# P V in four bursts per pair of heads, with no maxima in those steps

## The chip, the cores and the metric

The kernel runs on one core of one Trainium2 chip. A core has a matrix engine (TensorE, PE in the profile, with its weight loads shown apart as PEld), VectorE (DVE), ScalarE (ACT), GpSimd (POOL) and a queue for transfers (SyncE, SP). Each engine works through its own instructions in the order in which the program lists them, and waits for the others by semaphores. The metric is the device time of one execution in microseconds (us); three runs of the kernel before gave 1525.46, 1531.42 and 1532.0.

## What is computed

Attention with pooled queries, and behind it a mixture of experts with one expert per token:

```
q_pool = q.reshape(B, H, S // 2, 2, D).mean(axis=3)         # B=8, H=8, S=1152, D=64: 576 queries a head
scores = matmul(q_pool, k.transpose(0, 1, 3, 2)) / sqrt(D)
scores = scores - max(scores, axis=-1, keepdims=True)
attn   = exp(scores); attn = attn / (sum(attn, axis=-1) + 1e-9)
x      = matmul(attn, v)        # to [4608, 512]; then argmax gate, w1, relu, w2 and two gate factors per token
```

The change is in the attention, which takes the first 1020 us of some 1530; what follows is the experts' part, which the change does not touch.

## The kernel before

**The stages.** The 64 heads are worked off as 32 pairs, and the pairs one behind the other. A pair takes 18 steps: a step is one of the 9 key chunks of 128 keys of one of its two heads, so step 0 to 8 belong to the first head and 9 to 17 to the second (`s` in the code counts the steps of all pairs, and "step 4" below is `s % 18 == 4`). Three things run through the steps at different places of the program at once:

- *scores*: in each step the scores of this step's chunk, keys on the partitions and 576 queries in two halves of 288. Four matmuls of 288 columns (two at L394, two at L396) fill one of two PSUM buffers (`sps0`, `sps1`, by turns). The exponentials follow in one of two ways. On the GpSimd way ScalarE writes exp twice, once in f32 (`p32`, L408) and once in f16 (`ph`, L409), and GpSimd writes their difference, the low half `pl`, at L410. On the VectorE way (chunks listed in `PLP`) ScalarE writes `ph` (L400) and then exp over the scores in PSUM (L401), and VectorE takes the difference at L404 straight from PSUM. On this way the PSUM buffer comes free only after L404; on the other it comes free after L409. The scores two steps on need that buffer.
- *maxima*: for the *next* pair, the row maxima, 27 units a pair. A unit is two matmuls (three in some) of 384 columns at L331 into one of three small PSUM buffers, and a reduce by VectorE at L332. After 15 units, and after 27, the maxima are transposed on PE (L366), split on VectorE (L371, L372: `mr`) and sent by two transfers (L377 by way of L126), which ScalarE's queue issues, into the rows 66 and 67 of `qb`, where the scores matmul of the next pair subtracts them.
- *P V* (`av`): for a chunk whose `ph` and `pl` are there, 15 groups of weights with a matmul of 64 or 65 columns each (L425 to L427; 5 blocks of 128 queries, three products), accumulated over the 9 chunks of a head in one PSUM buffer. `ALAG` puts this 6 steps behind the scores. After the last chunk of a head VectorE normalizes (L434 to L436).

**What sets the order.** The loop at L657 writes the program step by step, and the order in which it calls things is the order on the engines: low halves and splits left over from the step before (`pendv`), router steps, one pending small job (`pop`), the scores, the maxima due, the transposes of maxima (`rows`, L679), then as many chunks of P V as `BURST` says for this step. The maxima due come from the line `mw`: one and a half units per step. `PREP` adds per pair, at fixed thirds of steps, the loading and splitting of the queries and keys two pairs ahead (on ScalarE, GpSimd and SyncE's queue) and the scaling of the values. Once in four pairs a router chain (L508) follows, which holds one of the three small PSUM buffers for several steps.

`BURST` has 9 bursts of 1 to 3 chunks a pair before. `PB` is the number of buffers for `ph` and for `pl`. The last pair of all has a list of its own, `PLPL`, and no maxima beside it.

Of the kernel before, what the change touches and what calls it, by code (L numbers as in the profile page):

```python
# [19 lines left out]
LEAD = 18  # L20
L0 = 18
LS = 0
# [5 lines left out]
         (78, 'amax', 0), (82, 'amax', 1), (99, 'gmax'), (100, 'scale', 0), (100, 'scale', 1), (100, 'scale', 2), (103, 'vh', 0), (103, 'vs', 0), (106, 'vh', 1), (107, 'vl', 0), (109, 'vs', 1), (113, 'vl', 1))  # L28
PREP = ((0, 'lk'), (12, 'kh', 0), (12, 'qsum'), (17, 'kh', 1), (18, 'kl'), (18, 'dk', 0), (19, 'dk', 1), (22, 'qh'), (24, 'dq', 0), (25, 'dq', 1), (26, 'ql'), (29, 'qd'), (30, 'dl', 0), (32, 'dl', 1),
        (63, 'lv'), (82, 'amax', 0), (88, 'amax', 1), (93, 'gmax'), (94, 'scale', 0), (95, 'scale', 1), (99, 'scale', 2), (100, 'vh', 0), (101, 'vs', 0), (103, 'vl', 0), (107, 'vh', 1), (107, 'vs', 1), (110, 'vl', 1))  # L30
BURST = {0: 2, 2: 2, 4: 2, 6: 2, 8: 1, 10: 2, 12: 2, 14: 2, 16: 3}
PLP = (1, 3, 7, 9, 11, 13)
PLPL = (1, 3, 5, 8, 11, 14, 17)
WSTEP = (8, 11, 14, 17)
IMM = 0
# [6 lines left out]
TS = 256  # L42
TLAG = 1
ALAG = 6
PB = 9
P32 = 6
SLEAD = 32
S = 1152
# [19 lines left out]
def attention(tc, qT, kT, vL, wg, keep, xrows, idscr, cum, pairs, setup, scat, init, exps):  # L68
    nc = tc.nc
    nb = len(pairs) // 4  # L70
    with ExitStack() as ctx:
# [53 lines left out]
        def dmaf(o, i, q=nc.sync):  # L125
            q.dma_start(out=o.bitcast(F32), in_=i.bitcast(F32))  # L126
# [220 lines left out]
        def pop(k=1):  # L347
            while k and fill:
                fill.pop(0)()
                k -= 1  # L350
# [3 lines left out]
        def sends():  # L354

            while pendd and pendd[0][1] < now[0]:
                pendd.pop(0)[0]()
# [3 lines left out]
        def rows(force=False):  # L361
            while pend_t and (force or now[0] >= pend_t[0][-1] + TLAG):
                m9, nt, t0, t1, qbf, _ = pend_t.pop(0)
                tp, tk = psum(True)
                tp = tp[0:nt, 0:128]
                nc.tensor.transpose(out=tp, in_=m9[:, 0:nt], identity=ident)  # L366
                mr = sm.tile([5, 2, 128], F32R, name="mr")[0:nt]
                c0 = 16.0 * SHIFT

                def split(tp=tp, tk=tk, mr=mr, qbf=qbf, t0=t0, t1=t1, nt=nt):  # L370
                    nc.vector.tensor_scalar(out=mr[:, 0], in0=tp, scalar1=c0, scalar2=None, op0=ALU.subtract)  # L371
                    nc.vector.scalar_tensor_tensor(out=mr[:, 1], in0=tp, scalar=c0, in1=mr.bitcast(F32)[:, 0], op0=ALU.subtract, op1=ALU.subtract)  # L372
                    free(tk)

                    def send():
                        for j in range(2):
                            dmaf(qbf[66 + j:67 + j, 128 * t0:128 * t1].rearrange("o (t n) -> o t n", n=128), mr[:, j], nc.scalar)  # L377
                    pendd.append((send, now[0]))
                if now[0] < 18:
                    split()  # L380
                else:
                    pendv.append(split)

        def scores(st, h):
            ka, kb, qa, qb = st['ka'], st['kb'], st['qa'], st['qb']
            o = h * (NQ + 64)
            for c in range(NC):
                ks = slice(128 * c, 128 * c + 128)
                ph = pp.tile([128, NQ], F16, name="ph", bufs=PB)
                pl = pp.tile([128, NQ], F16, name="pl", bufs=PB)  # L390
                st['ph', h, c], st['pl', h, c] = ph, pl
# [6 lines left out]
                ph2 = ph.rearrange("p (j n) -> p j n", j=2)  # L398
                if c + 9 * h in (PLP if st['n'] < LASTN else PLPL):
                    nc.scalar.activation(out=ph2, in_=x, func=AF.Exp, scale=1.0 / 16)  # L400
# [52 lines left out]
        def consts():  # L453
            nc.sync.dma_start(out=wf, in_=wg)
            nc.gpsimd.memset(wgt.bitcast(F32), 0.0)
            nc.gpsimd.tensor_copy(out=wgt[:, :, 0:16], in_=wf)
            nc.gpsimd.tensor_tensor(out=wgt[:, :, 16:32], in0=wf, in1=wgt.bitcast(F32)[:, :, 0:16], op=ALU.subtract)
            nc.gpsimd.iota(eoff, pattern=[[0, 5], [ESTRIDE, 8]], base=0, channel_multiplier=0, allow_small_or_imprecise_dtypes=True)
            for x in exg:
                nc.gpsimd.memset(x, 1e-9)  # L460
            nc.gpsimd.memset(moob, 0.0)
            nc.gpsimd.memset(moob[0:64, 4:5], float(OOB))
            make_lower(nc, tri)
            nc.gpsimd.memset(cum, 0.0)
# [153 lines left out]
        NP = len(pairs)  # L618
        pos = dict(m=0)

        def adv(k, g, want):
            while pos[k] < want:
                next(g, None)
                pos[k] += 1
# [3 lines left out]
        def prep_at(s, ph):  # L628
            u = 3 * (s + SLEAD) + ph
            for n in range(max(u // 54 - 2, 0), min(u // 54 + 2, NP)):  # L630
                r = u - 54 * n + min(3 * (LEAD - 15), 2 * n)
                if r == 0:
                    preps[n] = prep(n, PREP if n > 1 else PREP0 if n else PREPF)
                if n in preps:
                    for f in preps[n].pop(r, ()):
                        f()

        E = mybir.EngineType
        with tc.manual_schedule(engines={E.PE, E.DVE, E.Activation, E.Pool}):
            for s in range(-SLEAD, 0):  # L640
                for ph in range(3):
                    prep_at(s, ph)
                if s == -RI:
                    for i in (1, 2):
                        dmaf(QBs[i][64:66], QBs[0][64:66])
                        dmaf(KBs[i][64:68], KBs[0][64:68])
                if s == 1 - SLEAD + INIT:
                    consts()
                if s == -3:
                    init(0)  # L650
                if s >= -int(L0):
                    adv('m', mg, int(1.5 * (s + 1 + L0)))
                    now[0] = s
                    sends()
                    pop(3)
                    rows()
            for s in range(18 * NP + 14):  # L657
                now[0] = s
                live = s < 18 * NP
                if s % 18 == 2 and 0 < s // 18 < 5:  # L660
                    with tc.issue_after(lastk[0].ins):
                        init(s // 18)
                sends()
                while pendv:
                    pendv.pop(0)()
                for r in routers:
                    if not s % 2 or not live or not r[1]:
                        r[1] = next(r[0], 0)
                pop()
                if live:  # L670
                    next(sg)
                prep_at(s, 0)
                mw = min(27 * NP, int(1.5 * (s + 1 + min(LEAD, L0 + LS * s))))
                if pos['m'] < mw:
                    adv('m', mg, pos['m'] + 1)
                prep_at(s, 1)
                adv('m', mg, mw)
                if s < 54 or s % 2 == 0:
                    rows()  # L679
                if pos['m'] == 27 * NP:  # L680
                    pop(2)
                j = s - ALAG
                for _ in range(BURST.get(j % 18, 0) if 0 <= j < 18 * NP else 0):
                    next(ag)
                prep_at(s, 2)
                if not live:
                    pop(3)
            pop(99)
            for r in routers:
                for _ in r[0]: pass  # L690
# [456 lines left out]
def body(tc, qT, kT, vL, wg, w1, w2, out, nb=8):  # L1147
    nc = tc.nc
    NTOK = nb * NQ
    with tc.tile_pool(name="dram", bufs=1, space=bass.MemoryType.DRAM) as dp, tc.tile_pool(name="keep", bufs=1) as kp:  # L1150
        xrows = dp.tile([NTOK + 1, XW], F32, name="xrows")
        idscr = dp.tile([NID, IW], I32, name="idscr")
        cum = kp.tile([128, 8], BF16, name="cum")
        m = Moe(tc, kp, None, xrows, idscr, cum, w1, w2, out, nb)
        keep = m.keep = keep_tiles(tc, kp, m.NT, m.NU)
        di = kp.tile([128, 256], I32, name="di")

        def init(i):
            if i == 0:
                dz = kp.tile([1, XW], F32, name="dz")  # L1160
                nc.gpsimd.memset(dz, 0.0)
                nc.sync.dma_start(out=xrows[NTOK:NTOK + 1], in_=dz)
                nc.gpsimd.memset(di, NTOK)
                return
            r0, r1 = 5 * (i - 1), min(5 * i, NID * IW // 32768)
            ids = idscr.rearrange("(p r n) o -> p r (n o)", p=128, n=256 // IW)
            nc.sync.dma_start(out=ids[:, r0:r1], in_=di.unsqueeze(1).broadcast_to([128, r1 - r0, 256]))
        pairs = [(b, hp) for b in range(nb) for hp in range(4)]
        attention(tc, qT, kT, vL, wg, keep, xrows, idscr, cum, pairs, m.setup, m.scat, init, m.exps)
        m.run()  # L1170
# [32 lines left out]
```

## Time and profile before

| | |
|---|---|
| runs, us | 1525.46, 1531.42, 1532.0 (median 1531.42) |
| profiled execution, us | 1531.21, its span 1529.5 |
| granted TensorE clock, mean | 0.987 of full speed |
| PE busy (matmuls) | 1485.5 us, 97% of the span |
| ACT, DVE, POOL busy | 73%, 72%, 66% of the span |
| attention: scores of the first pair to those of the last chunk | 26 us to 1015 us |
| a pair without router work (493.42 to 523.54) | 30.12 us |

A row of a view has the line, the engine, the operation and what it writes from what it reads; times are us, "mean ns of one" is one instruction's duration. A matmul's duration is longer than its share of the engine, since matmuls overlap in the pipeline: what one costs is the distance from its start to the start of the next. The same holds for ACT and DVE, where an instruction starts some 0.1 us before the one ahead of it is recorded as ended.

### The profile page before, as it was taken

What the parts mean: (1) busy time and instruction counts of PE and PEld (TensorE: products, weight loads), DVE (VectorE), ACT (ScalarE), POOL (GpSimd) and SP (SyncE); (2) the same over time, 40 slices, a digit from 0 to 9 for tenths busy, and PEclk for the clock granted to TensorE, in tenths of its full rate; (3) what the DMA queues carried; (4) which work ended last, traced back from release to release, by engine and by line L of the source; (5) the groups of instructions that cost most, each with busy time, mean ns of one, the idle gap of its engine ahead of it and who ended that gap; (6) DMA issues with size and microseconds to landing.
All of it is one profiled execution on the core that took longest, in us unless ns stands there. A gap on an engine that the chain in (4) does not pass through costs nothing. (4 is left out here: it accounts for less than half of the span.)

```text
span 1529.5 us, 40884 instructions
## 1 busy us (share of the span) xinstructions
PE 1485.5 (97%) x15838; PEld 1347.8 (88%) x15838; DVE 1106.9 (72%) x2339; ACT 1123.0 (73%) x1949; POOL 1005.6 (66%) x889
## 2 busy tenths in 40 slices
PE   7999999999999999999999999979999999999998
PEld 6999999999999999999999899967888888888875
DVE  7677777776786777677777777647777777777762
ACT  5888888887888888888888888865565565565552
POOL 4887898788878888889878988766233233333210
PEclk9999999999999999999999999989999999999999
DMA  5577566665675566656765676065836666544550
GB/s 168 135 193 188 134 153 172 164 150 133 160 171 155 134 158 167 162 133 156 176 154 152 146 176 161 19 241 164 319 106 231 233 216 224 203 151 163 179 188 35
DMA packets 91984, 253.35 MB, mean 166 GB/s; under 512 B 12714, under 2 KB 16954, under 8 KB 91778
## 3 DMA queue, kind: packets, MB, share of 16 engines
q1 hardware_dynamic: 81194, 228.93, 53.5%
q0 software_dynamic: 9152, 20.85, 3.9%
q8 instruction: 129, 2.11, 0.6%
q10 hardware_dynamic: 1440, 0.89, 0.2%
q14 instruction: 69, 0.57, 0.1%
HBM read 164.23 MB, written 23.02 MB: 122 GB/s over the span
## 5 line engine op out<-in xcount | busy, mean ns | idle before, releaser
L332 DVE TENSOR_REDUCE pm<-mp 128x1 f32<-128x384 f32 x864 | 453.1, 551 | 219.5 <-PE mp L331 218.5
L410 POOL TENSOR_TENSOR pl<-p,ph 128x576 f16<-128x576 f32 x383 | 490.4, 1286 | 148.7 <-ACT ph L409 116.0
L408 ACT ACTIVATE p<-sps 128x576 f32<-128x576 f32 x383 | 250.7, 655 | 98.6 <-PE sps L396 58.8
L331 PE MATMUL mp<-ka,qa 128*128 128x384 f32 x960 | 315.1, 344 | 0.0
L425 PEld LDWEIGHTS <-ph 128*128 128x128 f16 x2880 | 263.2, 97 | 40.0 <-issue 28.9
L425 PE MATMUL av<-vt,ph 128*128 128x65 f16 x2880 | 296.4, 194 | 0.1
L426 PE MATMUL av<-vt,ph 128*128 128x64 f16 x2880 | 294.2, 195 | 0.0
L427 PE MATMUL av<-vt,pl 128*128 128x65 f16 x2880 | 293.3, 193 | 0.0
L394 PE MATMUL sps<-qa,ka 128*128 128x288 f32 x1152 | 279.8, 325 | 13.4 <-DVE pl L404 6.6
L426 PEld LDWEIGHTS <-ph 128*128 128x128 f16 x2880 | 265.9, 97 | 0.8
L427 PEld LDWEIGHTS <-pl 128*128 128x128 f16 x2880 | 266.1, 99 | 0.0
L331 PE MATMUL mp<-kb,qb 66*128 66x384 f32 x768 | 260.9, 340 | 0.9 <-DVE kb L205 0.6
L409 ACT ACTIVATE ph<-sps 128x576 f16<-128x576 f32 x383 | 249.4, 651 | 0.0
L396 PE MATMUL sps<-qb,kb 68*128 68x288 f32 x1152 | 248.6, 298 | 0.0
L905 PE MATMUL hps<-x,w1h 128*128 128x512 f32 (+1 forms) x704 | 233.3, 393 | 6.7 <-DVE x L889 4.2
L394 PEld LDWEIGHTS sps<-qa,ka 128*128 128x128 f32 x1152 | 185.0, 192 | 18.2 <-ACT ph L409 9.0
L396 PEld LDWEIGHTS sps<-qb,kb 68*128 68x128 f32 x1152 | 187.4, 191 | 0.0
L331 PEld LDWEIGHTS mp<-ka,qa 128*128 128x128 f32 x960 | 178.7, 190 | 1.8 <-DVE pm L332 1.5
L907 ACT COPY hs<-hps 128x512 f32<-128x512 f32 (+1 forms) x88 | 49.1, 558 | 174.0 <-PE hps L905 174.0
L905 PE MATMUL hps<-x,w1l 128*128 128x256 f32 (+1 forms) x704 | 167.0, 279 | 0.0
L404 DVE TENSOR_TENSOR pl<-sps,ph 128x576 f16<-128x576 f32 x193 | 145.9, 756 | 20.1 <-ACT sps L401 18.3
L400 ACT ACTIVATE ph<-sps 128x576 f16<-128x576 f32 x193 | 126.4, 655 | 41.1 <-PE sps L396 30.8
(231 smaller groups left out, 2948.0 us busy)
## 6 DMA issues: line engine op xcount, KB each, us to landing
ka<-xk SPq DMA_DIRECT2D x120, 288.0 KB
raw1b<-in_w_dram SPq DMA_DIRECT2D x24, 1024.0 KB
raw2b<-in_w_dram SPq DMA_DIRECT2D x24, 1024.0 KB
raw1a<-in_w_dram SPq DMA_DIRECT2D x22, 1024.0 KB
raw2a<-in_w_dram SPq DMA_DIRECT2D x22, 1024.0 KB
vp<-in_vL_dram SPq DMA_DIRECT2D x32, 576.0 KB
qp<-in_qT_dram SPq DMA_DIRECT2D x31, 576.0 KB
kpf<-in_kT_dram SPq DMA_DIRECT2D x31, 576.0 KB
```

The lines of the kernel that those rows point to most:

```text
L331: nc.tensor.matmul(mp, lhsT=l, rhs=r, start=j == 0, stop=j == len(ops) - 1)
L332: nc.vector.tensor_reduce(out=pm[:, i:i + 1], in_=mp, axis=AX.X, op=ALU.max)
L394: nc.tensor.matmul(sps[:, j, 0:288], lhsT=ka[:, h, ks], rhs=qa[:, o + 288 * j:o + 288 * j + 288], start=True, stop=False)
L396: nc.tensor.matmul(sps[:, j, 0:288], lhsT=kb[:, h, ks], rhs=qb[:, h, 288 * j:288 * j + 288], start=False, stop=True)
L404: nc.vector.tensor_tensor(out=pl.rearrange("p (j n) -> p j n", j=2), in0=x, in1=ph2, op=ALU.subtract)
L408: nc.scalar.activation(out=p32.rearrange("p (j n) -> p j n", j=2), in_=x, func=AF.Exp, scale=1.0 / 16)
L409: e_ = nc.scalar.activation(out=ph2, in_=x, func=AF.Exp, scale=1.0 / 16)
L410: nc.gpsimd.tensor_tensor(out=pl, in0=p32, in1=ph, op=ALU.subtract)
L425: nc.tensor.matmul(av_[:, qb, 0:65], lhsT=hi, rhs=vt[:, h, c, 0:65], start=c == 0 and qb == 0, stop=False)
L426: nc.tensor.matmul(av_[:, qb, 0:64], lhsT=hi, rhs=vt[:, h, c, 66:130], start=False, stop=False)
L427: nc.tensor.matmul(av_[:, qb, 0:65], lhsT=lo, rhs=vt[:, h, c, 0:65], start=False, stop=c == NC - 1 and qb == 4)
L905: nc.tensor.matmul(hp[:, f, 0:n], lhsT=W1[l][g][:, c, fs], rhs=d['x'][:, c, 0:n], start=c == 0 and l == 0, stop=c == 3 and l == 0)
```

## The change

Four tables are written anew:

```diff
-BURST = {0: 2, 2: 2, 4: 2, 6: 2, 8: 1, 10: 2, 12: 2, 14: 2, 16: 3}
-PLP = (1, 3, 7, 9, 11, 13)
+BURST = {3: 5, 8: 4, 12: 5, 17: 4}
+UNITS = (0, 2, 2, 2, 1, 0, 2, 2, 2, 0, 2, 2, 2, 2, 0, 2, 2, 2)
+PLP = (0, 4, 5, 9, 13, 14)
@@
-PB = 9
+PB = 10
@@ in the loop over the steps
-                mw = min(27 * NP, int(1.5 * (s + 1 + min(LEAD, L0 + LS * s))))
+                mw = min(27 * NP, 27 * (s // 18 + 1) + sum(UNITS[:s % 18 + 1]))
```

`BURST` is read with the lag of 6 steps, so the four bursts stand in steps 9 (5 chunks), 14 (4), 0 (5) and 5 (4); those are the steps with no unit of maxima in `UNITS`. The other steps have two units, step 4 one. The count of everything stays: 18 chunks of scores, 27 units, 18 chunks of P V and 6 low halves on VectorE a pair. One line is added to the file, so lines from L34 on are one higher in the changed kernel.

The order on PE about step 4 and 5 of a pair (scores are `sps`, maxima `mp`; the burst's first group is shown). Before, step 4:

```order
L394 MATMUL sps_10762<-qa_124,ka_121 128x288 x2
L396 MATMUL sps_10762<-qb_127,kb_118 128x288 x2
L331 MATMUL mp_10772<-ka_122,qa_125 128x384
L331 MATMUL mp_10772<-kb_119,qb_128 128x384
L425 LDWEIGHTS ph
L425 MATMUL av_10557<-vt_138,ph 128x65
```

The change, steps 4 and 5:

```order
L395 MATMUL sps_10748<-qa_124,ka_121 128x288 x2
L397 MATMUL sps_10748<-qb_127,kb_118 128x288 x2
L332 MATMUL mp_10756<-ka_122,qa_125 128x384
L332 MATMUL mp_10756<-kb_119,qb_128 128x384
L395 MATMUL sps_10763<-qa_124,ka_121 128x288 x2
L397 MATMUL sps_10763<-qb_127,kb_118 128x288 x2
L426 LDWEIGHTS ph
L426 MATMUL av_10589<-vt_138,ph 128x65
```

The burst has moved from step 4, behind a unit of maxima, to step 5, directly behind the scores.

VectorE at the same place, from the unit of step 4 to the units of step 6 (`pl` is a low half, `r` and `xb` the normalization at the end of a head). Before, where units stand in step 5 too:

```order
L332 TENSOR_REDUCE pm<-mp_10772 128x1
L434 TENSOR_SCALAR r<-av_10557,sc 128x5
L435 RECIPROCAL r<-r 128x5
L436 TENSOR_TENSOR xb<-av_10557,r 128x5x64
L332 TENSOR_REDUCE pm<-mp_10838 128x1
L332 TENSOR_REDUCE pm<-mp_10842 128x1
```

The change:

```order
L333 TENSOR_REDUCE pm<-mp_10756 128x1
L405 TENSOR_TENSOR pl<-sps_10748,ph 128x576
L405 TENSOR_TENSOR pl<-sps_10763,ph 128x576
L435 TENSOR_SCALAR r<-av_10589,sc 128x5
L436 RECIPROCAL r<-r 128x5
L437 TENSOR_TENSOR xb<-av_10589,r 128x5x64
L333 TENSOR_REDUCE pm<-mp_10848 128x1
L333 TENSOR_REDUCE pm<-mp_10852 128x1
```

Two low halves, of chunks 4 and 5, now stand ahead of the normalization and of the reduces behind it.

ScalarE in steps 3 to 5 (`qb<-mr` are the two transfers of maxima). Before:

```order
L400 ACTIVATE ph<-sps_10742 128x576
L401 ACTIVATE sps_10742<-sps_10742 128x2x288
L126 DMA qb_127<-mr 1x4x128 x2
L408 ACTIVATE p_10767<-sps_10762 128x576
L409 ACTIVATE ph<-sps_10762 128x576
L408 ACTIVATE p_10832<-sps_10827 128x576
L409 ACTIVATE ph<-sps_10827 128x576
```

The change:

```order
L409 ACTIVATE p_10732<-sps_10727 128x576
L410 ACTIVATE ph<-sps_10727 128x576
L127 DMA qb_127<-mr 1x4x128 x2
L401 ACTIVATE ph<-sps_10748 128x576
L402 ACTIVATE sps_10748<-sps_10748 128x2x288
L401 ACTIVATE ph<-sps_10763 128x576
L402 ACTIVATE sps_10763<-sps_10763 128x2x288
```

The transfers keep their place ahead of chunk 4; chunks 4 and 5 now go the VectorE way, and chunk 3 the GpSimd way.

## The prediction

> **What bounds the kernel now.** I read the page's first part, then four consecutive pairs by windows, then what PE waits for between 60 and 986 us, then the timelines of PE, ACT and DVE in one pair.
>
> ```profile
> span 1529.5 us, 40884 instructions
> PE 1485.5 (97%) x15838; PEld 1347.8 (88%) x15838; DVE 1106.9 (72%) x2339; ACT 1123.0 (73%) x1949; POOL 1005.6 (66%) x889
> ```
> ```profile
> core 0: us, PE busy (x) PEld busy (x) DVE busy (x) ACT busy (x) POOL busy (x), PEclk, DMA share, GB/s
> 493.42:523.54 30.12, 30.12 (x414) 28.72 (x413) 22.36 (x54) 26.21 (x49) 25.21 (x22) 1.00 0.63 152
> 523.54:554.55 31.01, 30.90 (x419) 29.17 (x418) 23.20 (x58) 26.08 (x49) 24.46 (x24) 1.00 0.58 147
> 554.55:585.55 31.00, 30.70 (x420) 28.81 (x419) 24.39 (x70) 26.57 (x51) 27.47 (x24) 1.00 0.68 163
> 585.55:617.08 31.53, 30.37 (x413) 28.67 (x412) 22.38 (x54) 25.96 (x49) 27.50 (x25) 1.00 0.64 155
> ```
> ```profile
> PE sps L394 <- ACT ph L409: 5.7, 6, 1.3
> PE tp L480 <- DVE pm L332: 2.4, 8, 0.3
> PE tp L497 <- DVE pm L332: 0.3, 1, 0.3
> ```
>
> The pair without router work (first window) has PE busy for all of its 30.12 us: PE's own instructions set its time, and no wait does. In 926 us PE's waits add up to 8.4 us. So a pair's time changes in two ways only: PE's instructions cost less, or another engine comes late. ACT and POOL have 26 and 25 us to do in the 30, DVE 22: little room for the first two.
>
> **What PE's instructions cost.** The timeline of PE in that pair, steps 4 and 5:
>
> ```profile
> 499.37 0.34 PE L331 MATMUL mp<-ka,qa 128*128 128x384 f32 x1
> 499.54 0.34 PE L331 MATMUL mp<-kb,qb 66*128 66x384 f32 x1
> 499.71 0.42 PE L394 MATMUL sps<-qa,ka 128*128 128x288 f32 x2
> 499.98 0.43 PE L396 MATMUL sps<-qb,kb 68*128 68x288 f32 x2
> 500.24 0.34 PE L331 MATMUL mp<-ka,qa 128*128 128x384 f32 x1
> 500.42 0.34 PE L331 MATMUL mp<-kb,qb 66*128 66x384 f32 x1
> 500.61 0.21 PE L425 MATMUL av<-vt,ph 128*128 128x65 f16 x1
> 500.65 0.19 PE L426 MATMUL av<-vt,ph 128*128 128x64 f16 x1
> ...
> 501.95 0.19 PE L427 MATMUL av<-vt,pl 128*128 128x65 f16 x1
> 501.98 0.51 PE L394 MATMUL sps<-qa,ka 128*128 128x288 f32 x2
> 502.33 0.43 PE L396 MATMUL sps<-qb,kb 68*128 68x288 f32 x2
> ```
>
> By distances of starts: a chunk's scores 0.53 us (499.71 to 500.24), a unit of maxima 0.35, three chunks of P V 1.37 (500.61 to 501.98), so 0.456 a chunk. Behind maxima the first two score matmuls take 0.27; behind P V they take 0.35. So each burst costs 0.08 us when it ends, and 0.01 when it begins (the first two P V matmuls are 0.04 apart, the others 0.03). The reading: the weights of the first f32 matmul load while the matmul ahead streams, and a P V matmul of 0.03 us hides little of that load.
>
> By the Trainium skill (TensorE: Matmul & The Clock Gate, Part 2, step by step) a 64-deep window pulls weight loads ahead of matmuls in flight; if that held without limit, a switch would cost nothing and the gain below would be 0. The rows above, 0.35 against 0.27, speak against it here. The same page's figure for 128 columns of weights (section on LDWEIGHTS) gives an estimate of 107 - 30 = 77 ns a switch and 12 us in all.
>
> **The gain.** 9 bursts become 4: 5 x 0.095 (0.083 + 0.012, the same distances in the trace's nanoseconds) = 0.475 us a pair, over 31 pairs 14.7 us. No matmul is added or removed. The tenth `ph` and `pl` buffer is needed by chunk 9, whose scores stand ahead of the first burst, and adds no work.
>
> **The waits that it adds.** The new order packs two units into 1.23 us steps (0.53 + 2 x 0.35) and leaves 0.88 us for step 4. I walk from step 2 (its start is 0). Steps 3, 4, 5 and 6 start at 1.34 (the transpose of maxima costs 0.11), 2.57, 3.45 and 5.81 (0.53 + 4 x 0.456), if nothing waits. The rows of ACT, then DVE, in the pair above:
>
> ```profile
> 499.22 0.65 ACT L400 ACTIVATE ph<-sps 128x576 f16<-128x576 f32 x1 [0.74 <-PE sps L396]
> 499.28 0.60 ACTq L126 DMA_DIRECT2D qb<-mr  x1
> 499.76 0.65 ACT L401 ACTIVATE sps<-sps 128x576 f32<-128x576 f32 x1
> 499.98 0.59 ACTq L126 DMA_DIRECT2D qb<-mr  x1
> 500.67 0.65 ACT L408 ACTIVATE p<-sps 128x576 f32<-128x576 f32 x1 [0.26 <-DVE pm L332]
> 501.21 0.65 ACT L409 ACTIVATE ph<-sps 128x576 f16<-128x576 f32 x1
> ```
> ```profile
> 497.97 0.55 DVE L332 TENSOR_REDUCE pm<-mp 128x1 f32<-128x384 f32 x1
> 498.43 0.27 DVE L371 TENSOR_SCALAR mr<-tp 4x128 fp32r<-4x128 f32 x1
> 498.74 0.28 DVE L372 SCALAR_TENSOR_TENSOR mr<-tp,mr 4x128 fp32r<-4x128 f32 x1
> 499.57 1.02 DVE L332 TENSOR_REDUCE pm<-mp 128x1 f32<-128x384 f32 x2 [0.56 <-PE mp L331]
> 500.52 0.76 DVE L404 TENSOR_TENSOR pl<-sps,ph 128x576 f16<-128x576 f32 x1
> 501.19 0.55 DVE L332 TENSOR_REDUCE pm<-mp 128x1 f32<-128x384 f32 x1
> 502.18 0.22 DVE L434 TENSOR_SCALAR r<-av,sc 128x5 f32<-128x5 f32 x1 [0.44 <-PE av L427]
> 502.44 0.19 DVE L435 RECIPROCAL r<-r 128x5 f32<-128x5 f32 x1
> 502.67 0.49 DVE L436 TENSOR_TENSOR xb<-av,r 128x320 f32<-128x320 f32 x1
> 503.14 1.02 DVE L332 TENSOR_REDUCE pm<-mp 128x1 f32<-128x384 f32 x2
> ```
>
> *First, the transfers of maxima.* Before, the split (L372) ends at 499.02, ahead of the exponentials (499.22), and both transfers are issued beside these; the next exponential starts 1.39 us after the first issue (499.28 to 500.67), a few tenths later than without them. Now two reduces stand ahead of the split. The first starts 0.38 after its second matmul (499.19 to 499.57): 0.53 + 0.18 + 0.38 = 1.09; the second 0.47 later, the split at 2.03, L372 at 2.34 to 2.62. The transfer waits for that on ACT, and chunk 4's exponentials are queued behind it: 2.65 + 1.39 = 4.04, though their scores are there at 2.57 + 0.73 = 3.30 (a chunk's scores start 0.73 ahead of its exponentials; the 0.81 of 498.41 to 499.22 has the 0.08 behind a burst).
>
> *Second, the scores of step 6.* They need chunk 4's PSUM buffer, which VectorE's low half frees: second exponential 4.58 to 5.23, L404 at 5.33 (0.11 after, as 500.41 to 500.52) to 6.09. PE is there at 5.81: a wait of about 0.3. Without the late transfers it would be free 0.4 ahead of PE.
>
> *Third, the units of step 6 and 7.* Chunk 5's exponentials are 1.08 behind chunk 4's, so its L404 starts at 6.42, the normalization at 7.09 (+0.67, as 500.52 to 501.19), the first reduce at 8.05 (+0.96, as 502.18 to 503.14). It frees its small buffer at 8.60; PE, at step 7 by 7.41, wants it for its second unit at 8.29: 0.3 more. The transposes of the finished head's output (L480) behind it need the second reduce: 0.1 more. Together 0.4. Before, no low half stood at this place, and the normalization found DVE idle.
>
> *Fourth, steps 14 to 16* have the same sequence: transfers, chunks 13 and 14 for VectorE, a normalization. But a 1.5 us step 13 and a burst of 1.83 us lie between, and the same walk leaves 0.1.
>
> So 0.3 + 0.4 + 0.1 = 0.8 of waits against 0.475: +0.325 us a pair, 30 x 0.325 = +10 us. Bounds: nothing, if the transfers cost ACT no more than now (the first of them issued 0.06 after an exponential, as at 499.28): then only the 0.1 stays, -0.375 a pair. Above, 1.3, if they are later by another 0.4, since every later item is then later by as much. I take the middle, since the walk is made of rows of one pair at full clock.
>
> *Router pairs.* In one pair of four the chain's 16 further VectorE instructions (54 to 70 in the windows) and one held small buffer meet the two-unit steps. With two buffers a step's units go round in 0.18 + 0.38 + 0.47 + 0.55 = 1.6 us from the first matmul to the second release, and PE comes back after 1.23 + 0.35 = 1.58: no reserve, where the old order had 1.65 us for 1.5 units. Bounds 0 to 2 us for each of 8; I take 3 us in all. *The end.* At the last scores 9 chunks of P V are left in place of 7: 2 x 0.456 = 0.9 us, and in the last pair, which has no maxima to fill PE, a burst of 2.3 us makes ACT wait for scores: I take 1.5 together, bounds 0.5 to 4.
>
> *Nothing changes* for POOL: its 12 low halves a pair stay, and between the last of a burst's chunks and its burst lie five steps, 7 us and more, against 1.3 us an instruction. The transfers of queries and keys keep their steps.
>
> Sum: 10 + 3 + 1.5 = 14.5, on the profiled execution's 1531.2 (span 1529.5), and this is 0.2 under the median of the runs: **1546 us**.
>
> **Rivals.** *The gain is kept*: the issues of the maxima's transfers don't hold chunk 4, because ACT or DVE stand earlier than in my walk, and DVE catches up in the bursts, in which it has no reduces. For it: the walk's first wait is 0.3 in a chain of ten links; against it: each link is a row. 31 x -0.375 + 1.5 = -10, 1521 us; without any wait 1518. *The two sides cancel*: the wait for chunk 4's buffer comes, but PE, now late, no longer meets the late reduces: 0.3 + 0.1 - 0.475 = -0.075 a pair, with router and end 1531 + 2 = 1533. *Router pairs pay more*, at their upper bound of 2 us: 8 x 2 in place of 3 gives 1559. For this: two buffers without reserve; against: the windows with router work are now 0.9 us longer than the one without, their own instructions counted.
>
> **Chances.** Forecast 0.4 (its own range 1539 to 1553), gain kept 0.25, cancel 0.25, router more 0.1. A change under 0.5% (7.7 us) can't be told from none here, so faster 0.25, same 0.25, slower 0.5. The range for 8 in 10: 1520 to 1557; below lies half of the gain case, above part of the router case.
>
> **What would show it.** In the changed kernel: score matmuls behind P V at 0.35 in 4 steps a pair and not 9 (right if the pair's PE instructions sum to 29.6); PE's wait at the scores of step 6 for VectorE's low half, some 30 times 0.3 us, as the first row of its waits; a wait for reduces in step 7; the first transfer of maxima issued 0.4 to 0.5 us after chunk 3's first exponential in place of 0.06. If pairs without router work take under 30.0 us, the walk is wrong, and the transfers' row shows where; if they take 30.4 and the whole is still unchanged, the router pairs or the end gained what I gave as lost.

## The result, and the profile after

The changed kernel took 1554.12, 1562.76, 1543.53 and 1556.69 us, median 1555.4; the kernel before, beside it, 1530.84 (four runs). The ratio is 1.0161, with a 95% interval of 1.0131 to 1.0191: slower by 1.6%, which is clear of the 0.5% that a measurement can tell. The profiled execution is the one of 1554.12.

In the changed kernel every line number from L33 on is one higher than in the kernel before (a table was added). The first part of its page:

```profile
span 1552.4 us, 40798 instructions
PE 1494.8 (96%) x15838; PEld 1355.3 (87%) x15838; DVE 1113.9 (72%) x2339; ACT 1110.3 (72%) x1949; POOL 1002.5 (65%) x889
```

Engine by engine the work is what it was, to within 13 us. What PE waited for between 60 and 986 us is not (columns: total us, times, longest):

```profile
PE sps L395 <- DVE r L435: 9.6, 7, 2.7
PE mp L332 <- DVE pm L333: 6.1, 11, 0.8
PE sps L397 <- issue: 1.7, 2, 1.5
PE tp L481 <- DVE pm L333: 1.6, 8, 0.3
```

Before, there were 8.4 us of waits in all, and none of the first two kinds. Both end at VectorE. "r L435" in the first row is only the instruction that VectorE ran last; what the scores need there is the low half ahead of it (shown below). The windows of the same four pairs as in the prediction, now in the changed kernel:

```profile
core 0: us, PE busy (x) PEld busy (x) DVE busy (x) ACT busy (x) POOL busy (x), PEclk, DMA share, GB/s
498.85:529.16 30.31, 30.18 (x413) 28.82 (x413) 22.50 (x54) 25.33 (x48) 24.35 (x22) 1.00 0.57 160
529.16:559.97 30.81, 30.81 (x418) 29.14 (x418) 23.35 (x58) 25.90 (x50) 25.21 (x24) 1.00 0.54 147
559.97:592.83 32.86, 31.22 (x419) 28.87 (x419) 24.71 (x70) 26.33 (x52) 27.15 (x24) 1.00 0.69 161
592.83:626.63 33.80, 31.32 (x414) 29.46 (x414) 22.76 (x54) 26.31 (x50) 28.61 (x26) 0.98 0.61 146
```

The first two pairs take what they took (30.12 and 31.01 before, 30.31 and 30.81 now). The third and the fourth take 1.9 and 2.3 us more. The pairs repeat with a period of four, so I sorted all of them by their number modulo 4 (the four windows are pairs 15, 16, 17 and 18, so remainders 3, 0, 1 and 2; in pairs of remainder 1 the router's chain stands). Seven of the eight pairs of remainder 1 take 1.1 to 2.6 us more than before; those of remainder 2 vary from 0.7 less to 4.1 more. Then I measured each step from its first score matmul to that of the next step. For each step the shortest time over pairs 2 to 29 is taken as what PE's instructions cost, and what the mean over pairs 4 to 30 of a kind has above it as waits (0.53 + 0.11 us in steps 15 and 16 of remainder 0 are router instructions of PE's own, in both kernels; so are 0.2 us in step 3 of remainder 1). This is worked out from the matmul records of the two profiled executions:

```
us per pair           steps 0-4   5     6     7    8-13   14    15    16    17 |  all    PE's instructions
before  n%4=1           0.36   0.00  0.05  0.53  0.01  0.20  0.00  0.00  0.00 | 1.16    29.86
        n%4=2           0.05   0.01  0.00  0.08  0.20  0.18  0.94  0.26  0.08 | 1.80
        n%4=3           0.02   0.00  0.01  0.01  0.02  0.20  0.04  0.03  0.00 | 0.33
        n%4=0           0.03   0.01  0.00  0.00  0.03  0.18  0.53  0.11  0.01 | 0.91
after   n%4=1           0.49   0.03  0.02  1.40  0.32  0.14  0.33  0.48  0.02 | 3.22    29.42
        n%4=2           0.27   0.11  0.02  0.20  0.31  0.35  1.27  0.50  0.39 | 3.42
        n%4=3           0.65   0.09  0.09  0.31  0.06  0.12  0.00  0.07  0.00 | 1.40
        n%4=0           0.15   0.04  0.02  0.24  0.06  0.12  0.54  0.11  0.16 | 1.45
```

and by stretches of the program, the sums of the pairs of a kind (pairs 1 to 30):

```
us              to end of pair 0   n%4=1 (8)  n%4=2 (8)  n%4=3 (7)  n%4=0 (7)   last pair and rest    span
before                60.31         247.45     252.01     211.21     215.39         543.13          1529.49
after                 58.27         258.74     260.84     214.93     216.06         543.56          1552.40
```

**So the gain is there and is paid away almost three times over.** PE's own instructions cost 0.44 us a pair less (29.86 to 29.42), which is 13 us over 30 pairs. The waits cost 38 us more in the same pairs (24.5 + 13.2), and two thirds of that stand at two places: step 7 (12 us over all pairs, 7 of them in the router's pair), and steps 14 to 17 of the router's pair and the pair after it (15 us). The rest lies in steps 0 to 6 and 8 to 13, a part of it at half clock (below).

**Place one, steps 14 to 17: ScalarE stands at a transfer, and VectorE's low half of chunk 14 is behind it.** The timeline of ScalarE in pair 18 of the changed kernel, then of VectorE, then of PE (start, duration, line, operation, and the idle time ahead with what ended it):

```profile
616.67 0.66 ACT L402 ACTIVATE sps<-sps 128x576 f32<-128x576 f32 x1
618.29 2.57 ACTq L127 DMA_DIRECT2D qb<-mr  x2
620.90 0.65 ACT L401 ACTIVATE ph<-sps 128x576 f16<-128x576 f32 x1 [3.58 <-PE mp L332]
621.45 0.65 ACT L402 ACTIVATE sps<-sps 128x576 f32<-128x576 f32 x1
```
```profile
622.13 0.76 DVE L405 TENSOR_TENSOR pl<-sps,ph 128x576 f16<-128x576 f32 x1 [3.29 <-ACT sps L402]
```
```profile
620.36 0.34 PE L332 MATMUL mp<-kb,qb 66*128 66x384 f32 x1
623.03 0.50 PE L395 MATMUL sps<-qa,ka 128*128 128x288 f32 x2 [2.33 <-DVE r L435]
```

ScalarE ends chunk 13's exponentials at 617.33 and does none until 620.90. Between them stand the two transfers of maxima, issued at 618.29 and 620.17. Chunk 14's scores had been ready since about 617.3 (step 14 starts at 616.72). Its low half ends at 622.89, and PE starts chunk 16's scores in that buffer at 623.03. What ScalarE waits for in those 3 us is told by the semaphore records of the trace: the first transfer uses the completion semaphore that a transfer `ka<-xk` of SyncE's queue had used before it, the second that of a `qa<-xq`, and each is issued 0.08 us after the 16th and last increment of that earlier transfer (618.21 and 620.09). SyncE issued those long before:

```profile
607.87 3.95 SPq L127 DMA_DIRECT2D ka<-xk  x4
611.92 0.85 SPq L127 DMA_DIRECT2D qa<-xq  x1
```

Fifteen of the `ka<-xk` transfer's increments came by 616.57, the sixteenth 1.64 us later. By the Trainium skill (DMA: Bandwidth & Descriptors, on why a DMA increments its semaphore by 16) only all sixteen mean that the data has landed; the records agree, since ScalarE moved at the sixteenth each time.

That is so in most pairs of remainders 1 and 2. There the second transfer of this batch is issued 1.7 and 2.5 us after the split that it sends (means over pairs 4 to 30), in remainders 3 and 0 after 0.65 and 0.55.

Before, the same wait stood in the pairs of remainder 2 (0.94 + 0.26 in steps 15 and 16). ScalarE in pair 18 of the kernel before:

```profile
610.58 1.97 ACTq L126 DMA_DIRECT2D qb<-mr  x2
612.60 0.65 ACT L408 ACTIVATE p<-sps 128x576 f32<-128x576 f32 x1 [2.58 <-DVE r L435]
```

But there chunk 14 went the GpSimd way: its PSUM buffer was free when ScalarE was done, and not 0.8 us later, after VectorE (622.10 to 622.89 above).

**The clock behind such a wait.** Windows of the changed kernel around it; PEclk is the granted clock:

```profile
619.21:623.03 3.82, 1.49 (x14) 1.20 (x11) 0.89 (x2) 2.13 (x4) 0.22 (x1) 1.00 0.88 198
623.03:625.20 2.17, 2.03 (x12) 1.71 (x13) 2.11 (x7) 1.46 (x4) 1.31 (x2) 1.00 0.92 285
625.20:628.60 3.40, 3.40 (x28) 3.25 (x28) 1.77 (x5) 2.41 (x5) 3.40 (x4) 0.50 0.07 27
```

For 3.40 us the clock is 0.50, which costs up to 1.7 us (an estimate: half of 3.40). Between 60 and 1000 us there are 17 us at half clock after the change (behind three such pairs: 10, 18 and 22) and 3.4 before: up to 6.8 us of the 24.5.

**Place two, step 7: the reduces of step 6 stand behind everything else on VectorE.** VectorE in pair 17 of the changed kernel, and PE at the same time:

```profile
570.27 0.76 DVE L405 TENSOR_TENSOR pl<-sps,ph 128x576 f16<-128x576 f32 x1
570.95 0.20 DVE L569 TENSOR_REDUCE tp<-exg 128x5 f32<-128x45 f32 x1
...
571.49 0.18 DVE L435 TENSOR_SCALAR r<-av,sc 128x5 f32<-128x5 f32 x1
...
571.93 0.49 DVE L437 TENSOR_TENSOR xb<-av,r 128x320 f32<-128x320 f32 x1
572.34 1.01 DVE L333 TENSOR_REDUCE pm<-mp 128x1 f32<-128x384 f32 x2
```
```profile
571.91 0.42 PE L397 MATMUL sps<-qb,kb 68*128 68x288 f32 x2
572.95 0.44 PE L332 MATMUL mp<-ka,qa 128*128 128x384 f32 x1 [0.61 <-DVE pm L333]
```

Step 6's units were multiplied by 571.64, but chunk 5's low half, three router instructions and the normalization come first, and the router holds the third small buffer. So step 7's first unit waits for the first reduce, and its second for the second.

### The profile page after: what moved, and what is told of

It is laid out like the page before. It is cut to its first block, busy times and chain, and to the rows that moved or that the text cites. A ratio compares the mean times of both kernels' runs of the same rounds, so it can differ in the third digit from the quotient of the medians.

```text
span 1552.4 us, 40798 instructions
## 1 busy us (share of the span) xinstructions
PE 1494.8 (96%) x15838; PEld 1355.3 (87%) x15838; DVE 1113.9 (72%) x2339; ACT 1110.3 (72%) x1949; POOL 1002.5 (65%) x889
## 4 chain that ended last, share of the span: by engine, by line
PE 86%; DVE 7%; ACT 3%; DMA 2%; issue 1%; ACTq 0%; POOL 0%; SPq 0%; DVEq 0%; POOLq 0%
PE mp L332 18%; PE hps L906 15%; PE sps L395 9%; PE sps L397 9%; PE av L427 5%; PE av L426 5%; PE av L428 5%; PE yp L930 4%; PE yp L929 4%; PE yp L928 4%; DVE pm L333 3%; DMA qa<-xq 2%; PE tp L481 1%; PE yp L926 1%; DVE pl L405 1%
## 5 line engine op out<-in xcount | busy, mean ns | idle before, releaser
L333 DVE TENSOR_REDUCE pm<-mp 128x1 f32<-128x384 f32 x864 | 442.0, 548 | 73.2 <-PE mp L332 66.9
L332 PE MATMUL mp<-ka,qa 128*128 128x384 f32 x960 | 322.2, 352 | 7.2 <-DVE pm L333 6.1
L409 ACT ACTIVATE p<-sps 128x576 f32<-128x576 f32 x383 | 251.0, 655 | 106.1 <-PE sps L397 82.7
L395 PE MATMUL sps<-qa,ka 128*128 128x288 f32 x1152 | 271.1, 317 | 18.9 <-DVE r L435 9.6
L426 PE MATMUL av<-vt,ph 128*128 128x65 f16 x2880 | 282.7, 194 | 0.0
L428 PE MATMUL av<-vt,pl 128*128 128x65 f16 x2880 | 281.2, 193 | 1.1 <-issue 1.0
L427 PE MATMUL av<-vt,ph 128*128 128x64 f16 x2880 | 281.7, 195 | 0.1
L395 PEld LDWEIGHTS sps<-qa,ka 128*128 128x128 f32 x1152 | 192.8, 192 | 31.5 <-issue 9.9
```

The lines of the kernel that those rows point to most:

```text
L332: nc.tensor.matmul(mp, lhsT=l, rhs=r, start=j == 0, stop=j == len(ops) - 1)
L333: nc.vector.tensor_reduce(out=pm[:, i:i + 1], in_=mp, axis=AX.X, op=ALU.max)
L395: nc.tensor.matmul(sps[:, j, 0:288], lhsT=ka[:, h, ks], rhs=qa[:, o + 288 * j:o + 288 * j + 288], start=True, stop=False)
L409: nc.scalar.activation(out=p32.rearrange("p (j n) -> p j n", j=2), in_=x, func=AF.Exp, scale=1.0 / 16)
L426: nc.tensor.matmul(av_[:, qb, 0:65], lhsT=hi, rhs=vt[:, h, c, 0:65], start=c == 0 and qb == 0, stop=False)
L427: nc.tensor.matmul(av_[:, qb, 0:64], lhsT=hi, rhs=vt[:, h, c, 66:130], start=False, stop=False)
```

## Experiments

Every run is compared with the kernel before on the same chip; the tables above are made for each in the same way. Beside experiments 1 to 3 the kernel before took 1526.6 us, beside 4 to 6 1527.3 and beside 7 1530.0, while the expectations, in absolute times, were worked out from 1531. So a time can stand up to 4 us lower than on the scale of its expectation, and the ratio decides. In the expectations, lo(14) is the low half of chunk 14.

**1. The old places of the low halves, with the new bursts.**

```diff
-PLP = (0, 4, 5, 9, 13, 14)
+PLP = (1, 3, 7, 9, 11, 13)
```

> The changed kernel with PLP as it was before (chunks 1, 3, 7, 9, 11, 13 of a pair on the VectorE way), bursts and maxima as changed. Theory 1, that the place of VectorE's low halves costs the time (lo(14) behind the transfers of maxima on ACT's queue, lo(5) ahead of the reduces): the waits of steps 14 to 17 go, and the time is 1520 to 1530, below the kernel before by some of the 0.475 us a pair that fewer bursts give. Theory 2, that packing the maxima two to a step costs it, with reduces late whatever stands beside them: 1550 or more. Theory 3, the walk on record: both have a share, 1535 to 1548.

Measured: 1591.3 us, 1.0412 (1.0372 to 1.0452). Theory 1 falls by 60 us, and the walk's 1535 to 1548 with it. Only theory 2's bound holds, and its reason (late reduces) is not what the trace shows: the first row of PE's waits in this run is for low halves.

```profile
PE sps L395 <- DVE pl L405: 27.0, 62, 1.2
```

In pair 15 of this run VectorE's and PE's timelines show the place, step 4 and the scores behind it. The 62 waits of the row stand behind steps 4, 8 and 2 (22, 20 and 20 of them), few of them in the router's pairs.

```profile
522.41 1.00 DVE L333 TENSOR_REDUCE pm<-mp 128x1 f32<-128x384 f32 x2
523.34 0.73 DVE L405 TENSOR_TENSOR pl<-sps,ph 128x576 f16<-128x576 f32 x1
```
```profile
523.23 0.34 PE L332 MATMUL mp<-kb,qb 66*128 66x384 f32 x1
524.22 0.51 PE L395 MATMUL sps<-qa,ka 128*128 128x288 f32 x2 [0.65 <-DVE pl L405]
```

Where a step packs two units into 1.23 us, a low half queues behind two reduces (1.0 us), and the scores two steps on want its buffer. The new places are needed by the new bursts; taken as a whole they are not what costs the time.

**2. The new places with the old bursts.**

```diff
 # the kernel before, with
-PLP = (1, 3, 7, 9, 11, 13)
+PLP = (0, 4, 5, 9, 13, 14)
```

> The kernel before with the new PLP alone (chunks 0, 4, 5, 9, 13, 14 on the VectorE way), bursts and maxima as they were. Theory 1 (the place of the low halves costs it, whatever the bursts): 1540 to 1550. Theory 2 (the packing of maxima and bursts costs it): 1529 to 1534. If the new places hurt only together with the new bursts: within 4 us of the kernel before.

Measured: 1566.2 us, 1.0245 (1.0205 to 1.0285), far over every expectation, so none of the three stands as written. The largest rows of PE's waits:

```profile
PE sps L396 <- DMA qb<-mr: 13.2, 6, 4.0
PE sps L394 <- DVE r L434: 6.2, 11, 1.1
```

PE waits for low halves here too (behind steps 6 and 15), and in pairs of remainder 2 step 0 waits 3.1 us for late rows of maxima. So each half of the change alone is worse than both together.

**3. The transfers of maxima on SyncE's queue.** One edit, in the changed kernel and, as a control, in the kernel before:

```diff
-dmaf(qbf[...], mr[:, j], nc.scalar)
+dmaf(qbf[...], mr[:, j])
```

> The changed kernel, its two transfers of maxima per batch issued on SyncE's queue instead of ACT's. If the losses are ACT standing at these transfers (chunk 4 and chunk 14 queued behind them): PE's waits for lo(14), about 10 us in the attention, go, with the clock dips behind them, and the time is 1535 to 1543. If VectorE's own order costs the time (reduces behind the low halves in steps 6 and 7): the waits at step 7 stay, and the time is within 4 us of the changed kernel, 1551 to 1559. SyncE's queue also carries the loads for later pairs; should the transfers hold those up, the pairs' first steps wait and the time is above 1560.

> The kernel before, its transfers of maxima issued on SyncE's queue. A control for the run above: the kernel before waits 1.3 us a router-driven pair in steps 15 to 17; if those waits are ACT standing at the transfers, 1520 to 1526; if the transfers cost nothing in the kernel before, 1529 to 1533; if SyncE's queue is the wrong place, above 1535.

Measured: the changed kernel 1541.9 us, 1.0092 (1.0061 to 1.0124), within the 1535 to 1543 that was given for ScalarE standing at the transfers (by the ratio 1545, just above it); the kernel before 1535.8, 1.0060 (1.0033 to 1.0086), worse, as given for "the wrong place". PE's waits in the first of the two:

```profile
PE sps L397 <- DMA qb<-mr: 13.2, 11, 2.1
PE mp L332 <- DVE pm L333: 5.1, 8, 0.8
```

The 9.6 us for chunk 14's low half are gone. In pairs of remainder 1 steps 15 and 16 fall from 0.81 to 0.02 us above the shortest, in those of remainder 2 steps 14 to 17 from 2.51 to 0.15. This shows place one: ScalarE's standing at the transfers is what PE waited for. Step 7 of remainder 1 stays (1.40 and 1.42), so place two has a cause of its own. And there is a new price: on SyncE's queue the rows come later, and step 0 of the next pair waits for them, 0.89, 1.12 and 0.56 us in remainders 2, 3 and 0. In the control steps 15 and 16 of remainder 2 fall from 1.20 to 0.01, and step 0 of remainder 3 goes from 0 to 2.19. Before the change as after it, the wait in those pairs can be moved but not removed in this way.

**4. The transfers on GpSimd's queue**, in the changed kernel and in the kernel before (`nc.gpsimd` in place of `nc.scalar`).

> The changed kernel, its transfers of maxima issued on GpSimd's queue. With SyncE's queue the waits of steps 15 to 17 went, but step 0 then waited 1.12, 0.89 and 0.56 us in three of four pairs for late rows, 17 us in all. If only the place of issue did that, both losses go: 1537 - 17 = 1520, so 1516 to 1526. If the transfers wait for something that holds them up on any queue, step 0 waits here too: 1534 to 1545. If GpSimd, standing at them, makes the low halves late: above 1545, with P V waiting for pl.

> The kernel before with its transfers of maxima issued on GpSimd's queue, the control for the first run of this set. If ACT standing at the transfers costs the kernel before its 1.28 us in steps 15 to 17 of every fourth pair, and GpSimd has room: 7 to 10 us less, 1516 to 1524. If step 0 then waits for late rows as with SyncE's queue: 1529 to 1537. If GpSimd has no room: above 1537.

Measured: 1604.0 us, 1.0524 (1.0484 to 1.0564), and 1548.3, 1.0137 (1.0102 to 1.0172). Both come out where I had put "GpSimd has no room", but not for that reason: PE does not wait for `pl`, it waits for the rows, in the changed kernel

```profile
PE sps L397 <- DMA qb<-mr: 48.7, 25, 4.1
```

GpSimd issues the second transfer of a batch 2.1 to 4.0 us after the split (means of the four kinds of pairs, batch of steps 13 to 17), where ScalarE does it after 0.6 to 2.3. Step 0 waits 2.4 to 3.8 us in three of four pairs. The rest is the transfer itself: in the semaphore records the last increment of the second transfer comes 6.1 us after its issue (median of the batches of steps 13 to 17 in pairs 4 to 30), on ScalarE's queue after 3.6, and in 24 of those 27 batches PE's scores of the next step 0 go on less than 0.3 us behind it.

**5. Chunk 14 on the GpSimd way**, and nothing else.

```diff
-PLP = (0, 4, 5, 9, 13, 14)
+PLP = (0, 4, 5, 9, 13)
```

> The changed kernel with chunk 14 on the GpSimd way (five chunks on VectorE instead of six), transfers on ACT's queue as changed. If the extra loss in steps 15 to 17 is chunk 14's low half on VectorE coming behind ACT's transfers: steps 15 to 17 fall to what they were in the kernel before (n%4=1: from 0.83 to about 0; n%4=2: from 2.16 to 1.3), 13 us less: 1538 to 1545. If the transfers alone cost it, whichever way the chunk takes: 1552 to 1558. If GpSimd is short of time for a 13th chunk: above 1556.

Measured: 1538.1 us, 1.0064 (1.0040 to 1.0088), within the first expectation (by the ratio 1541). Steps 14 to 17 of remainder 2 fall from 2.51 to 1.31 (before the change 1.46), steps 15 and 16 of remainder 1 from 0.81 to 0.39. Remainder 2's eight pairs take 252.5 us in place of 260.8, and the kernel before 252.0. ScalarE stands nearly as long as in the changed kernel, here in pair 18:

```profile
609.49 2.75 ACTq L127 DMA_DIRECT2D qb<-mr  x2
612.34 0.65 ACT L409 ACTIVATE p<-sps 128x576 f32<-128x576 f32 x1 [3.01 <-PE sps L397]
```

but PE waits 0.89 us for the buffer and not 2.33. GpSimd has room for the 13th chunk. One entry of one table is worth 15 of the 23 us by which the span had grown (1552.4 to 1537.4); the ratios, 1.0161 and 1.0064, say the same 15.

**6. Chunk 5 on the GpSimd way.**

```diff
-PLP = (0, 4, 5, 9, 13, 14)
+PLP = (0, 4, 9, 13, 14)
```

> The changed kernel with chunk 5 on the GpSimd way (VectorE: 0, 4, 9, 13, 14). If lo(5) and the normalization ahead of the reduces cost step 7 its time: 1.40 falls to about 0.5 in pairs behind a router step and 0.2 to 0.3 to about 0 in the others, 8 x 0.9 + 22 x 0.25 = 13 us less: 1540 to 1546. If the normalization and the router's VectorE work alone do it: step 7 stays and the time is 1550 to 1558. If the kept buffer was freed sooner by the VectorE way, step 7's scores wait and the time is above 1558.

Measured: 1549.2 us, 1.0149 (1.0123 to 1.0175), between the first expectation and the second (by the ratio 1554, in the second), and half of each holds. By the spans that is 7 us, by the ratios 2, so the steps tell more than the time. Step 7 falls from 1.40 to 0.81 in remainder 1 (0.5 expected), from 0.31 and 0.24 to 0.14 and 0.00 in remainders 3 and 0. So chunk 5's low half is some 0.6 us of place two in the router's pair. In this run's timeline the router's instructions and the normalization still stand ahead of the reduces; the last edit of experiment 7 takes the rest further apart.

**7. Both chunks on the GpSimd way, then two more edits on top of each other.**

```diff
-PLP = (0, 4, 5, 9, 13, 14)
+PLP = (0, 4, 9, 13)
```

> The changed kernel with chunks 5 and 14 both on the GpSimd way (VectorE: 0, 4, 9, 13). If the two losses are separate, they add: chunk 14 away gave 17 us and chunk 5 away 7 in the spans, of which 1 us stands in the same steps: 1552 - 17 - 6 = 1529, so 1524 to 1533, step 7 as with chunk 5 away and steps 15 to 17 as with chunk 14 away. If GpSimd with 14 chunks a pair becomes short (its low halves late, P V waiting for pl): above 1538, the time without chunk 14 alone.

Measured: 1537.3 us, 1.0033 (1.0012 to 1.0053). By the ratios that is 0.3% below the run without chunk 14 (1.0064), so the second edit gave some 5 us of the 6 given; the median is above the 1524 to 1533, whose sum had 17 us for chunk 14 where the spans have 15. Step 7 is as in experiment 6 (0.86), but steps 15 and 16 of remainder 2 are 1.48 against 0.77 in experiment 5. GpSimd, at 71% of the span, makes PE wait nowhere.

```diff
-for _ in range(BURST.get(j % 18, 0) ...):
+for _ in range((BURST if j < 18 * (NP - 1) else BURSTL).get(j % 18, 0) ...):   # BURSTL: the old list
```

> The kernel of the run above, with the old list of bursts for the last pair, which has no maxima beside it. The last pair took 3.0 us more than before in the changed kernel. If the four bursts did that: the last pair's steps go back from 31.6 to about 28.6 us and the time is 3 us below the run above. If it comes from what runs ahead of the last pair: no difference beyond 1.5 us.

Measured: 1534.1 us, 1.0024 (1.0006 to 1.0042), not to be told from the run above. The last pair takes 30.9 us against 32.5 there, 31.6 in the changed kernel and 28.6 before; in the next run, with the same list, it takes 32.2. The four bursts are not what lengthened it. What did is open; it matters little, since the last pair and all behind it together take 543.6 after the change and 543.1 before.

```diff
-UNITS = (0, 2, 2, 2, 1, 0, 2, 2, 2, 0, 2, 2, 2, 2, 0, 2, 2, 2)
+UNITS = (0, 2, 2, 2, 2, 0, 2, 1, 2, 0, 2, 2, 2, 2, 0, 2, 2, 2)
```

> The kernel of the run above, with one unit of maxima moved from step 7 to step 4 (2 and 1 there instead of 1 and 2). In pairs behind a router step the second unit of step 7 waits 0.8 us, since its small buffer is the one that step 6's last reduce frees. If the packing two by two at that place, with a buffer held by the router, makes the wait: it goes in these pairs, 8 x 0.8 = 6 us below the run above. If VectorE is late whatever the units: the wait appears at step 8 instead and the time is the same within 2 us.

Measured: 1528.0 us against 1530.0 for the kernel before, 0.9988 (0.9966 to 1.0009); by the ratios 5.5 us below the run above, where 6 were given. The eight pairs of remainder 1 take 242.6 us in place of 251.0. Step 7 of remainder 1 falls from 0.86 to 0.13, and step 8 gets 0.13. The pair that took 31.00 us before (the third window of the prediction) and 32.86 after the change takes in this kernel

```profile
547.10:577.44 30.34, 30.34 (x420) 29.05 (x419) 23.54 (x68) 25.86 (x51) 28.71 (x25) 1.00 0.68 165
```

with PE busy all the time. So the second unit at step 7, with the reduces late and a third small buffer held by the router, was the other part of place two. This version gives back what the change lost; it does not beat the kernel before by more than its measurement can tell. Left in it are 2.66 us of waits in pairs of remainder 2 (1.80 before), half of them in steps 15 to 17, where ScalarE still stands at its transfers.

## Why the prediction was right, and where it was not

**Time, sign and chances.** 1546 us were predicted, with 1520 to 1557; 1555.4 came, 24.6 us more than before where 14.5 were summed. Slower was the likeliest case, and it happened. The range held it with under 2 us to spare, nearer to the case of router pairs at their upper bound (1559) than to the forecast.

**The gain**: right. 0.475 us a pair were worked out, 0.44 is what the step table shows, with a pair's PE instructions at 29.42 (29.6 predicted). The score matmuls behind a burst are still 0.35 us apart. The rule of the Trainium skill on the 64-deep window (TensorE: Matmul & The Clock Gate, Part 2), taken without limit as the prediction did, would have made it 0; the measured 0.44 speaks against that reading for this sequence.

**First, the transfers, and second, the scores of step 6**: wrong, by one link. The walk let the first transfer wait for the second split (L372 of the kernel before). But it sends `mr[:, 0]`, which the first split (L371) writes alone. Pair 16 of the changed kernel, in which step 2 starts at 533.29; ScalarE, then VectorE, then PE:

```profile
535.43 0.65 ACT L409 ACTIVATE p<-sps 128x576 f32<-128x576 f32 x1 [0.16 <-POOL pl L411]
535.61 0.60 ACTq L127 DMA_DIRECT2D qb<-mr  x1
...
536.95 0.65 ACT L401 ACTIVATE ph<-sps 128x576 f16<-128x576 f32 x1 [0.33 <-DVE pm L333]
```
```profile
535.31 0.27 DVE L372 TENSOR_SCALAR mr<-tp 4x128 fp32r<-4x128 f32 x1
535.62 0.28 DVE L373 SCALAR_TENSOR_TENSOR mr<-tp,mr 4x128 fp32r<-4x128 f32 x1
...
538.24 0.76 DVE L405 TENSOR_TENSOR pl<-sps,ph 128x576 f16<-128x576 f32 x1 [0.69 <-ACT sps L402]
539.28 0.76 DVE L405 TENSOR_TENSOR pl<-sps,ph 128x576 f16<-128x576 f32 x1 [0.28 <-ACT sps L402]
```
```profile
539.18 0.51 PE L395 MATMUL sps<-qa,ka 128*128 128x288 f32 x2
```

Issued 2.32 after the start of step 2 (2.65 walked), 0.18 after chunk 3's first exponential (0.4 to 0.5 predicted); chunk 4's exponentials at 3.66 (4.04), its low half done at 5.71 (6.09), PE there at 5.89 (5.81). The buffer is free 0.18 us ahead of PE, so the wait of 0.3 us, 30 times, which was to be the first row of PE's waits, is not there. Step 5, in which it would show, has 0.03 to 0.11 us a pair. All later links of the walk hold to about 0.1 us once the 0.38 is taken off.

**Third, the reduces of step 7**: the place is right, the size was off. 0.4 us were given for each pair; it is 0.20 to 0.31 in three kinds of pairs (0.00 to 0.08 before), since chunk 5's low half also came 0.43 earlier, and 1.40 (0.53 before) in the router's pair, where experiments 6 and the last of 7 took it apart.

**Fourth, steps 14 to 16**: 0.1 was given, "the same walk leaves 0.1". That is the step that failed most. In remainders 3 and 0 it is right: steps 14 to 17 cost there what they did before. In remainders 1 and 2 it is 0.97 and 2.51 against 0.20 and 1.46 before. The walk knew that the transfers stand on ScalarE's queue ahead of chunk 14, but took them to be issued as soon as the split was done, as in the pair without router work from which the rows came. In most pairs of remainders 1 and 2 they wait for older transfers of SyncE's queue. Experiment 3 (the waits go when the transfers go) and experiment 5 (15 us go when only chunk 14's way is changed) show it.

**Router pairs**: 3 us in all, with bounds of 0 to 2 us for each of 8. Measured, the waits of remainder 1 rose by 2.06 us a pair (16 in all) and those of remainder 2 by 1.62 (13). The sum had 0.8 for every pair, so beyond it stand 1.26 and 0.82 a pair, 10 and 7 us. These are the terms that were mis-sized: the first is within its bounds but three times what was taken, and the other, the pair behind the router's, was not in the sum at all.

**The end**: 1.5 us, measured 0.4, with 2.0 gained ahead of pair 1. **The clock** was not in the sum: up to 6.8 us at half clock behind the long waits.

So the range held, but with a sum made of other parts, and that is in part luck. The wait of the second step, 9 us in the sum, is not there; step 7, 12 us in the sum and 3 more for the router's pairs, costs 12; steps 14 to 17, 3 us in the sum, cost 15. The first error hid most of the last. In remainders 3 and 0 the waits rose by 1.07 and 0.54 us a pair, where 0.8 was given; of the 1.07, though, 0.52 is step 0 at half clock behind the pair of remainder 2, and most of the rest is step 7. In the sixteen pairs of remainders 1 and 2 they rose by 29 us (8 x 2.06 + 8 x 1.62), where 16 x 0.8 + 3 = 16 were given. In the rivals, "the gain is kept" has the right link for the plain pairs (ScalarE's transfers do not hold chunk 4), and "router pairs pay more" is what happened to the whole.

## What to carry to other kernels

When work is packed more tightly, walk every kind of pair and not only the clean one, and ask of each moved instruction what it now stands behind on its engine: here a low half that was moved behind two transfers cost 15 us, while with the same low half on GpSimd those 15 us are gone. A transfer that ScalarE issued here waited not only for its data but also for the transfer that had used its completion semaphore before (618.21 to 618.29 above), and everything behind it on ScalarE waited with it; look for such a wait wherever a computing engine issues transfers. No run gave these transfers semaphores of their own, so what that would be worth is not shown. Read the waits by kind of pair and by step: the totals of the profile (8.4 us before, some 20 after) gave neither the place nor the cause, the table by step gave both.

## What the runs showed that I had not expected

- Two 2.5 KB transfers on ScalarE's queue kept that engine idle for 3.6 us. The first stood until the sixteenth increment of a 288 KB transfer issued 9.1 us earlier (609.07 to 618.21), the second until that of a 144 KB transfer issued 8.2 us earlier (611.92 to 620.09); each sixteenth came 1.64 us after the fifteenth. Why the last of sixteen parts comes so late, no run here shows.
- A wait of PE that is shorter than the 3.4 us at half clock can still bring them: 2.33 us of waiting (620.7 to 623.03), then 2.2 us of work at full clock, then 3.40 us at 0.50. By the Trainium skill (TensorE: Matmul & The Clock Gate, on why it matters for kernels) gaps of more than about 3 us are to be avoided; here a gap of 2.33 with 0.14 us of others behind it (the window from 619.21 to 625.20 has PE busy for 3.52 of 5.99 us) was enough. The waits of 1.98 and 2.73 us in pairs 10 and 22 brought half clock too, one of 1.51 us in pair 5 did not.
- Neither other queue was better for two rows of 2.0 to 2.5 KB: behind SyncE's loads the rows came up to 2.1 us too late for the next pair, and from GpSimd's queue up to 4.1.
